# Windowed attention with a mixture of adapters on one core: pooled PSUM banks, single output groups, a written order, and the regroup copies of q and k on GpSimd

## The chip, the cores and the metric

The kernel runs on one core of a Trainium2 chip. A core has five engines that run side by side, each working through its own list in order: TensorE (PE in the profile; its weight loads, PEld, overlap its matmuls), VectorE (DVE), ScalarE (ACT), GpSimd (POOL) and SyncE (SP). In this kernel GpSimd issues every load and SyncE every store. Matrix products land in PSUM, which has 8 banks of 2 KB per partition; the other tiles lie in SBUF. The metric is the device time of one execution in microseconds, lower is better, as a median of several runs.

## The reference

Sliding-window attention over 8 batches and 8 heads, 576 positions, head size 64, and behind it a mixture of 8 adapters of rank 16 of which each row takes two:

```python
scores = scale * np.matmul(q, k.transpose(0, 1, 3, 2))
mask = np.abs(pos[:, None] - pos[None, :]) <= 32
attn = softmax(np.where(mask, scores, -1e9))
x = np.matmul(attn, v)                 # heads side by side: 4608 rows x 512
logits = x @ w_gate                    # 8 gates a row, the two largest kept, softmax over them
out = x + sum over the two kept e of w_e * (x @ A[e]) @ B[e]
```

## The kernel before, in words

The work is a list of small tasks, each with a two-letter name. A planner (`tasks`, `plan`) gives each task an engine, an assumed cost, what it depends on and a due time, schedules them on a model of the engines, and the kernel then emits them in that order. Each engine's instructions keep the order in which they are emitted, so this order is what decides who waits behind whom.

Two heads at a time are worked on: a unit `u` is one pair of heads of one batch, 32 units in all, four to a batch.

- `LD` loads a tile of 128 rows of q (`w` = 0) or k (`w` = 1), 18 tiles each, in tile `l`, cast to f16 on the way (L272). A tile that lies across two batches takes two DMAs. Six buffers each. `LV` loads half a batch of v (L279), and `SV` shifts a part of it to other partitions (L284, VectorE).
- `RG`, the regroup copy (L288): the tile holds one head of the pair behind the other; the copy, SBUF to SBUF, puts the two heads of a position side by side (tile `c`, three buffers each).
- `TR` turns `c` by eight transposes on TensorE into PSUM (L296). `EQ` copies the turned q into the ring `qR` (L305 to L309), `EK` the turned k into the ring `kR` as two copies of 64 partitions (L316, ScalarE).
- `SC` makes a tile of eight score blocks: two matmuls of 512 columns for the mask (L323) and eight score matmuls (L327). `EX` is the exponential on ScalarE (L332), into tile `PT`.
- `PV` multiplies with v and a column of ones, 13 matmuls a unit (L346); `MU` divides by the sums, a reciprocal and a product on VectorE (L355, L356), into `x`.
- Once a batch: `TX` turns `x` (L368) and `XE` copies it to `xT` (L374); `PZ` multiplies with A and the gate weights (L382); `G1`, `GA`, `G2` choose the two gates and scale (L399 to L420, on VectorE but for one exponential at L407); `TZ` and `ZE` turn the scaled result (L427, L431); `PD` multiplies with B and adds x back through the identity (L437, L440), for two groups of 128 rows at a time; `OB` copies to the output tile `ob` (L449, ScalarE) and `ST` stores it (SyncE), one store for each group of rows.

PSUM is held as three tiles `W` of two banks for scores, PV, PZ and PD, and two tiles `T` of one bank for the transposes. A batch has five groups of 128 rows, so the output of a batch goes in three steps, of two, two and one group. `ZK`, `ZV`, `ZP` write the zeros and ones that stay in `kR`, `vbd` and `PT`. The weights of the adapters are loaded by six DMAs from GpSimd behind the 16th load (L507 to L511). The constants (identity, mask) are made on GpSimd when the first transpose is emitted.

Of the kernel before, what the change touches and what calls it, by code (L numbers as in the profile page):

```python
# [49 lines left out]
class Task:  # L50
    __slots__ = ("key", "eng", "cost", "deps", "take", "give", "due", "start", "end",
                 "left", "users", "ready", "slot", "lat", "seq")

    def __init__(self, key, eng, cost, deps, take=None, give=None, lat=0.2):
        self.key, self.eng, self.cost, self.deps = key, eng, cost, deps
        self.take, self.give, self.lat = take, give, lat


OFF = {"LD": -14.73, "LV": -10.97, "RG": -16.63, "TR": -2.72, "EQ": -37.15, "EK": 25.79, "SV": 12.6,
       "SC": -0.11, "EX": 11.83, "PV": 1.3, "MU": -33.19, "TX": 3.53, "XE": -49.66, "PZ": 7.11,  # L60
       "G1": -57.49, "GA": 7.42, "G2": -66.76, "TZ": -23.09, "ZE": 10.68, "PD": 11.21, "OB": 13.67,
       "ZK": 4.21, "ZV": 30.71, "ZP": 29.46}


def tasks(off=OFF):

    ts = {}

    def add(key, u, eng, cost, deps, take=None, give=None, lat=0.2):
        t = Task(key, eng, cost, deps, take, give, lat)  # L70
        t.due = u + off[key[0]]
        t.seq = len(ts)
        ts[key] = t

# [482 lines left out]
```

## Time and profile before

| | us |
|---|---|
| median of three runs | 145.97 (145.54 to 146.17) |
| profiled execution | 147.01 |
| its span, first to last instruction | 145.0 |
| TensorE busy in the span | 119.1 |
| ScalarE busy | 111.0 |
| VectorE busy | 109.9 |
| GpSimd busy | 52.0 |

All profile lines come from one execution. "L288" is line 288 of the kernel; behind a line stand the engine, the operation, what it writes and reads, and the shapes (partitions x elements). In a group, "x36 | 14.6, 434 | 5.4 <-DMA l" is: 36 instructions, 14.6 us busy in all, 434 ns each on average, and 5.4 us for which the engine stood idle ahead of them, mostly for the load of `l`. In the timeline the first number is the start and the second how long it took. Matmuls run pipelined, so a single busy time overlaps the next one. GpSimd's DMA rows show the time to issue a load, not the transfer.

### The profile page before, as it was taken

What the parts mean: (1) busy time and instruction counts of PE and PEld (TensorE: products, weight loads), DVE (VectorE), ACT (ScalarE), POOL (GpSimd) and SP (SyncE); (2) the same over time, 40 slices, a digit from 0 to 9 for tenths busy, and PEclk for the clock granted to TensorE, in tenths of its full rate; (3) what the DMA queues carried; (4) which work ended last, traced back from release to release, by engine and by line L of the source; (5) the groups of instructions that cost most, each with busy time, mean ns of one, the idle gap of its engine ahead of it and who ended that gap; (6) DMA issues with size and microseconds to landing.
All of it is one profiled execution on the core that took longest, in us unless ns stands there. A gap on an engine that the chain in (4) does not pass through costs nothing.

```text
span 145.0 us, 4013 instructions
## 1 busy us (share of the span) xinstructions
PE 119.1 (82%) x1624; PEld 100.9 (70%) x1624; DVE 109.9 (76%) x279; ACT 111.0 (77%) x127; POOL 52.0 (36%) x80
## 2 busy tenths in 40 slices
PE   0257959796789599999999999999999999792770
PEld 0246757685677598888979788988898788582440
DVE  5769889993895989899899999989778456946000
ACT  7739877569769569999998999889979975553160
POOL 7998377589534355546256021000000000000000
PEclk9999999999999999999999999999999999999558
DMA  2999999999999999999999999924403050548035
GB/s 10 204 141 183 199 198 188 132 128 142 163 195 180 190 243 207 198 283 229 223 209 276 195 216 280 178 58 156 133 0 127 16 188 5 192 136 300 28 127 199
DMA packets 38770, 24.12 MB, mean 166 GB/s; under 512 B 24800, under 2 KB 34144, under 8 KB 38752
## 3 DMA queue, kind: packets, MB, share of 16 engines
q0 software_dynamic: 33504, 14.43, 84.1%
q1 hardware_dynamic: 5248, 9.44, 19.0%
q8 instruction: 12, 0.20, 0.5%
q14 instruction: 6, 0.05, 0.1%
HBM read 28.85 MB, written 9.44 MB: 264 GB/s over the span
## 4 chain that ended last, share of the span: by engine, by line
PE 51%; DVE 24%; issue 10%; DMA 8%; ACT 2%; POOL 1%; ACTq 0%; DVEq 0%; POOLq 0%
PE W L346 10%; DMA l<-in_q_dram 8%; PE W L323 7%; PE W L327 7%; PE T L296 6%; PE W L437 5%; PE W L382 5%; PE W L440 5%; PE T L368 4%; DVE x L356 4%; DVE c L288 4%; DVE vbd L284 3%; DVE xT L374 3%; DVE rc L355 2%; DVE zs L420 2%
## 5 line engine op out<-in xcount | busy, mean ns | idle before, releaser
L316 ACT COPY kR<-T 64x1024 f16<-64x1024 f16 x36 | 36.2, 1005 | 7.1 <-PE T L296 6.8
L332 ACT ACTIVATE PT<-W 128x1024 f16<-128x1024 f32 x36 | 35.4, 1038 | 5.5 <-PE W L327 4.6
L346 PE MATMUL W<-vbd,PT 128*128 128x130 f16 x416 | 28.6, 219 | 2.0 <-DVE vbd L284 2.0
L296 PE MATMUL T<-ident,c 128*128 128x128 f16 x288 | 22.6, 229 | 9.0 <-DVE c L288 7.7
L449 ACT COPY ob<-W 128x1024 f32<-128x1024 f32 (+1 forms) x24 | 20.9, 876 | 9.9 <-PE W L440 7.7
L356 DVE TENSOR_TENSOR x<-W,rc 128x640 f16<-128x640 f32 x32 | 26.4, 824 | 1.1
L346 PEld LDWEIGHTS <-PT 128*128 128x128 f16 x416 | 25.0, 97 | 2.3 <-DVE vbd L284 2.3
L327 PEld LDWEIGHTS <-kR 128*128 128x128 f16 x288 | 19.5, 99 | 8.9 <-issue 0.7
L296 PEld LDWEIGHTS <-c 128*128 128x128 f16 x288 | 18.7, 103 | 9.7 <-DVE c L288 9.6
L323 PE MATMUL W<-identQ,mask 128*128 128x512 f16 x72 | 22.0, 387 | 2.7 <-DVE x L356 2.7
L327 PE MATMUL W<-qR,kR 128*128 128x128 f16 x288 | 22.4, 222 | 0.0
L272 POOL DMA_DIRECT2D l<-in_k_dram x24 | 15.9, 665 | 10.5 <-DMA l<-in_k_dram 3.1
L279 POOL DMA_DIRECT2D vbd<-in_v_dram x16 | 13.3, 835 | 16.0 <-PE T L427 7.4
L272 POOL DMA_DIRECT2D l<-in_q_dram x24 | 16.4, 683 | 7.0 <-DMA l<-in_k_dram 1.9
L288 DVE COPY c<-l 128x1024 f16<-128x1024 f16 x36 | 14.6, 434 | 5.4 <-DMA l<-in_k_dram 4.5
L440 PEld LDWEIGHTS <-xT 128*128 128x128 f16 x160 | 13.3, 104 | 7.1 <-issue 2.8
L437 PE MATMUL W<-B_sb,zT 128*128 128x512 f16 x40 | 16.4, 410 | 1.8 <-ACT zT L431 0.8
L374 DVE COPY xT<-T 128x1024 f16<-128x1024 f16 (+1 forms) x24 | 13.4, 598 | 4.6 <-PE T L368 3.8
L440 PE MATMUL W<-ident,xT 128*128 128x128 f16 x160 | 16.7, 231 | 0.0
L368 PE MATMUL T<-ident,x 128*128 128x128 f16 x160 | 11.8, 219 | 3.0 <-DVE xT L374 1.5
L284 DVE COPY vbd<-vbd 32x2304 f16<-32x2304 f16 x16 | 12.7, 794 | 0.7 <-DMA vbd<-in_v_dram 0.3
L368 PEld LDWEIGHTS <-x 128*128 128x128 f16 x160 | 9.8, 98 | 3.6 <-DVE x L356 1.7
(49 smaller groups left out, 115.5 us busy)
## 6 DMA issues: line engine op xcount, KB each, us to landing
out_dram<-ob SPq DMA_DIRECT2D x24, 256.0 KB, 2.9
vbd<-in_v_dram POOLq DMA_DIRECT2D x16, 288.0 KB, 9.4
l<-in_q_dram POOLq DMA_DIRECT2D x12, 256.0 KB, 9.6
l<-in_k_dram POOLq DMA_DIRECT2D x12, 256.0 KB, 9.9
out_dram<-ob SPq DMA_DIRECT2D x16, 192.0 KB, 2.9
l<-in_q_dram POOLq DMA_DIRECT2D x4, 192.0 KB, 7.6
l<-in_k_dram POOLq DMA_DIRECT2D x4, 192.0 KB, 7.3
l<-in_q_dram POOLq DMA_DIRECT2D x4, 128.0 KB, 9.1
```

The lines of the kernel that those rows point to most:

```text
L272: keep(nc.gpsimd.dma_start(out=raw[w][t % NRAW][f - FT * t:f - FT * t + n], in_=src[f - NF * b:f - NF * b + n]))
L296: keep(nc.tensor.matmul(out=tp[:, FT * slot:FT * slot + FT], lhsT=src[:, j, :], rhs=ident, is_transpose=True, start=True, stop=True))
L316: keep(nc.scalar.copy(out=dst.rearrange("p a (r f j) -> p a r f j", r=2, j=4), in_=kt[64 * o:64 * o + 64]))
L323: keep(nc.tensor.matmul(out=p[:, i:i + 4], lhsT=maskT, rhs=bcast(identQ, 1, 4), start=True, stop=False))
L327: keep(nc.tensor.matmul(out=p[:, i], lhsT=kR[:, a, :], rhs=qR[:, :, 8 * a:8 * a + 16], start=False, stop=(i % 4 == 3)))
L332: keep(nc.scalar.activation(out=PTs[T % NPT][:, :, 64:192].rearrange("p i (f j) -> p i f j", j=J), in_=ps("SC", T).rearrange("p (i j f) -> ...
L346: keep(nc.tensor.matmul(out=po[:, GS * g:GS * g + 2 * VD], lhsT=PTs[T % NPT][:, sl, off:off + 128], rhs=rhs[:, :, V0 - 1:V0 + D], start=(i ...
L356: keep(nc.vector.tensor_tensor(out=xs[b % NX].rearrange("p g (h n d) -> p g h n d", h=2, n=NP)[:, :, :, n], in0=pog[:, :, :, 1:VD], in1=bc ...
L368: keep(nc.tensor.matmul(out=tp[:, c0:c0 + 128], lhsT=xs[b % NX][:, g, 128 * c:128 * c + 128], rhs=ident, is_transpose=True, start=True, st ...
L437: keep(nc.tensor.matmul(out=pd[:, i], lhsT=zTs[b % 2][:, g], rhs=B_sb, start=True, stop=False))
L440: keep(nc.tensor.matmul(out=pd[:, i, 128 * c:128 * c + 128], lhsT=xTs[b % NXT][:, g, c], rhs=ident, start=False, stop=(c == 3)))
L449: keep(nc.scalar.copy(out=dst, in_=src))
```

## The change

- **Order.** The planner goes. A fixed text `ORDER` names the tasks in the order of emission. Behind a colon stands the PSUM bank (0 to 7) that a TensorE task writes, or the engine (A for ScalarE, D for VectorE) of a copy.
- **PSUM.** Four tiles of two banks serve everything; each task takes the bank or the pair of banks that `ORDER` names.
- **Regroup copies.** `RG` of tiles 0 and 1 stays on VectorE; the other 32 run on GpSimd, in the queue that also issues the loads.
- **Buffers.** Load tiles 4 in place of 6 for each of q and k, `xT` 3 in place of 2, and the output 7 tiles of one group in place of 3 of two.
- **Engines.** `EQ` is 14 times on VectorE and 4 times on ScalarE (9 and 9 before); of the 36 copies of `EK` 4 are on VectorE, and the two halves are separate tasks; `XE` is 16 times on VectorE and 10 on ScalarE (24 and 0); `ZE` in halves both ways; `ZV` 3 and 3.
- **Output.** `PD`, `OB` and `ST` go by single groups: 29 output copies on ScalarE and 11 on VectorE.
- **Last batch.** `MU` of the last unit, `PZ`, the scaling, `TZ` and `ZE` come in two parts (groups 0 to 2, then 3 and 4); `TX` and `XE` by single groups; and the residual matmuls (`PX`) come ahead of the product with B (`PB`).
- **Start.** The identity is made ahead of the first load; the other constants and the weights' loads have places of their own in the order. One gate step (`is2`, L414 before) moves from G2 to G1.

```diff
-NV, NPT, NRAW, NCAST, NX, NXT, NOB = 3, 4, 6, 3, 2, 2, 3
-NW, NTP = 3, 2
+NV, NPT, NRAW, NCAST, NX, NXT, NOB = 3, 4, 4, 3, 2, 3, 7
+NW = 4
+LB = B - 1
...
+ORDER = """
+CI ZK.1 LD.0.0 LD.0.1 ZP.0 LD.1.0 ZP.3 ZV.1.0:A LV.0.0 ZP.2 ZP.1 LD.1.1 Z1.1 Z1.2 CQ ZK.3 CM
+ZV.0.0:A RG.0.0 WB ZK.0 TR.0.0:0 LD.2.0 ZV.1.1:D EQ.0:A RG.1.0 LD.2.1 ZV.2.0:A RG.0.1 TR.1.0:0
+ZK.4 LV.0.1 TR.0.1:1 Z1.0 RG.1.1 WA EQ.1:D EK.0.0:A TR.1.1:2 ZV.0.1:D EK.0.1:A SV.0.0 EK.1.1:A
+SC.0:0 ZK.2 EK.1.0:A RG.2.0 SC.1:4 ZV.2.1:D EX.0 SC.2:2 RG.2.1 SV.0.1 EX.1 TR.2.0:6 LD.3.0
+TR.2.1:7 EQ.2:D LD.3.1 EX.2 PV.0:4 EK.2.1:D LD.4.0 SC.3:0 EK.2.0:A MU.0 PV.1:2 LV.1.0 EX.3
+SC.4:6 LV.1.1 MU.1 PV.2:0 RG.3.0 EX.4 MU.2 RG.3.1 TR.3.0:6 PV.3:2 EQ.3:D RG.4.0 TR.3.1:0 MU.3
+SC.5:6 EK.3.1:A LD.4.1 SV.1.0 TX.0.1:1 EX.5 TX.0.2:2 LD.5.0 TX.0.0:3 XE.0.2:D TR.4.0:4 XE.0.1:A
+LD.5.1 XE.0.0:D LV.2.0 EQ.4:D EK.3.0:A PZ.0:2 LD.6.0 SV.1.1 SC.7:0 G1.0 RG.4.1 PV.4:4 EX.7
+RG.5.0 TR.4.1:6 MU.4 GA.0 SC.6:0 EK.4.0:A RG.5.1 G2.0 TR.5.0:7 EX.6 LD.6.1 TR.5.1:4 EK.4.1:A
+PV.6:0 EQ.5:D LV.2.1 PV.5:2 EK.5.0:A MU.6 RG.6.0 SC.8:6 EK.5.1:A SV.2.0 LD.7.0 TZ.0:5 SC.9:0
+MU.5 ZE.0:A LD.7.1 TR.6.0:4 EX.8 RG.6.1 PD.0.1:5 EQ.6:D SC.10:2 EX.9 LD.8.0 SV.2.1 TR.6.1:4
+LD.8.1 EX.10 PV.7:6 EK.6.1:D LV.3.0 SC.11:0 OB.0.1:A RG.7.0 EK.6.0:A MU.7 ST.0.1.1 PV.8:2 RG.7.1
+EX.11 TR.7.0:5 MU.8 TX.1.2:4 TX.1.1:6 RG.8.0 EQ.7:A TX.1.0:7 XE.1.1:D TR.7.1:2 RG.8.1 XE.1.0:A
+XE.1.2:D SC.12:0 PV.9:4 LD.9.0 EX.12 PZ.1:6 LD.9.1 MU.9 EK.7.1:A LD.10.0 PV.10:0 G1.1 LD.10.1
+EK.7.0:A PD.0.2:3 LV.3.1 SC.13:4 OB.0.2:A MU.10 LV.4.0 GA.1 TR.8.1:2 ST.0.2.2 EX.13 G2.1
+TR.8.0:3 RG.9.0 SC.14:0 EK.8.1:A RG.9.1 PV.11:4 EQ.8:D EX.14 TZ.1:6 RG.10.0 MU.11 PD.0.3:7
+ZE.1:A PD.0.0:3 PD.0.4:0 RG.10.1 SV.3.0 OB.0.0:A TX.2.0:1 OB.0.4:A TX.2.1:6 ST.0.0.0 XE.2.0:D
+LV.5.0 EK.8.0:A TX.2.2:3 ST.0.4.4 SC.15:4 XE.2.2:D LV.5.1 XE.2.1:D OB.0.3:A TR.9.0:3 EX.15
+LV.4.1 SV.3.1 TR.9.1:2 ST.0.3.3 SC.16:6 EQ.9:D LD.11.0 EK.9.1:A PV.13:4 SV.4.0 EX.16 LD.11.1
+PV.12:0 MU.13 TR.10.1:3 EK.9.0:A PZ.2:6 LD.12.0 MU.12 EK.10.0:A LD.12.1 SC.17:4 LD.13.0 G1.2
+EK.10.1:A PD.1.2:2 TR.10.0:0 LD.13.1 OB.1.2:D GA.2 PD.1.1:1 EX.17 G2.2 PD.1.4:3 ST.1.2.7
+PD.1.0:2 LD.14.0 OB.1.4:A PV.15:4 RG.11.0 OB.1.0:A ST.1.4.9 PD.1.3:3 OB.1.1:A EQ.10:D ST.1.0.5
+TZ.2:2 RG.11.1 OB.1.3:A SC.18:6 ST.1.1.6 SV.4.1 ZE.2:A ST.1.3.8 PV.14:0 RG.12.0 MU.15 EX.18
+TR.11.1:2 TR.11.0:3 RG.12.1 MU.14 EK.11.1:A SC.19:6 EQ.11:D RG.13.0 TX.3.0:0 EX.19 SV.5.1
+TX.3.2:1 TX.3.1:3 LD.14.1 SC.20:4 XE.3.2:D XE.3.1:A RG.13.1 XE.3.0:D PV.16:6 EX.20 SV.5.0
+RG.14.0 SC.21:0 MU.16 PV.17:4 EX.21 LV.6.0 EK.11.0:D TR.12.1:3 RG.14.1 PZ.3:6 EK.12.1:A MU.17
+LD.15.0 PV.18:0 EK.12.0:A G1.3 PD.2.1:2 LD.15.1 TR.12.0:4 OB.2.1:A PD.2.0:5 MU.18 GA.3 SC.22:2
+ST.2.1.11 EQ.12:A LD.16.0 G2.3 TR.13.0:0 LD.16.1 OB.2.0:A PD.2.2:1 EX.22 LD.17.0 ST.2.0.10
+SC.23:4 RG.15.0 EQ.13:D TZ.3:6 EX.23 PV.19:2 OB.2.2:D RG.15.1 TR.13.1:7 ZE.3:D ST.2.2.12 PV.20:4
+MU.19 EK.13.1:A LV.7.1 SC.24:0 RG.16.0 MU.20 TX.4.0:6 EX.24 TX.4.2:2 RG.16.1 SV.6.0 TX.4.1:3
+PD.2.3:4 XE.4.0:A XE.4.1:D TR.14.0:5 LV.7.0 PD.2.4:0 XE.4.2:D OB.2.3:A TR.14.1:6 EQ.14:D RG.17.0
+OB.2.4:A PV.21:2 ST.2.3.13 EK.14.1:A EK.13.0:D ST.2.4.14 LD.17.1 SC.25:4 LV.6.1 EK.14.0:A PZ.4:0
+MU.21 EX.25 SV.7.1 SC.27:6 G1.4 PV.22:4 EX.27 RG.17.1 SC.26:2 MU.22 GA.4 SC.28:6 EX.26 G2.4
+TR.15.0:4 EX.28 TR.16.0:5 PD.3.2:2 EQ.16:D TR.15.1:3 EQ.15:A TZ.4:6 OB.3.2:D PD.3.4:7 PD.3.1:5
+EK.15.0:A ZE.4:D ST.3.2.17 PV.23:0 OB.3.4:D EK.15.1:A PD.3.3:2 SV.6.1 ST.3.4.19 SC.29:6 OB.3.3:A
+MU.23 PD.3.0:4 EX.29 ST.3.3.18 PV.24:2 OB.3.1:D TX.5.0:0 OB.3.0:A MU.24 ST.3.1.16 TX.5.2:1
+TX.5.1:5 ST.3.0.15 XE.5.2:A PV.25:6 XE.5.0:D XE.5.1:A TR.16.1:1 MU.25 SC.30:2 EK.16.0:A SV.7.0
+PZ.5:4 EX.30 PD.4.0:0 EK.16.1:A G1.5 PV.26:2 OB.4.0:A SC.31:6 MU.26 GA.5 ST.4.0.20 PD.4.2:0
+EX.31 G2.5 TR.17.1:1 PD.4.4:2 OB.4.2:A PD.4.3:3 OB.4.4:A PV.27:6 ST.4.2.22 OB.4.3:A ST.4.4.24
+TZ.5:0 MU.27 EK.17.1:A SC.32:4 ST.4.3.23 TR.17.0:3 EX.32 TX.6.2:2 EQ.17:D TX.6.1:6 TX.6.0:7
+XE.6.1:A XE.6.2:D SC.33:4 XE.6.0:D EK.17.0:A PV.28:2 PZ.6:6 EX.33 MU.28 ZE.5:A PD.4.1:1 G1.6
+PV.29:2 OB.4.1:A SC.34:4 ST.4.1.21 MU.29 GA.6 SC.35:0 EX.34 G2.6 PD.5.0:2 EX.35 PV.30:4 PD.5.2:3
+OB.5.0:A MU.30 TZ.6:0 OB.5.2:A PV.31:6 ST.5.0.25 ZE.6:D ST.5.2.27 PD.5.1:4 MA.31 PD.5.4:5
+OB.5.1:A PD.6.0:0 MB.31 OB.5.4:A TX.7.0:1 ST.5.1.26 OB.6.0:D TX.7.1:4 TX.7.2:6 ST.5.4.29
+XE.7.1:A TX.7.4:7 XE.7.0:D TX.7.3:5 ST.6.0.30 PD.5.3:0 XE.7.2:D XE.7.3:A PD.6.1:1 OB.5.3:D
+XE.7.4:A PZa.7:2 OB.6.1:A ST.5.3.28 PZb.7 ST.6.1.31 PD.6.2:1 G1.7 PD.6.4:0 OB.6.2:A PX.7.0:6
+OB.6.4:D ST.6.2.32 PX.7.1:4 GA.7 G2a.7 PD.6.3:1 ST.6.4.34 G2b.7 TZa.7:0 ZEa.7:D TZb.7:2 OB.6.3:D
+ZEb.7:A PB.7.0 PB.7.1 OB.7.0:A OB.7.1:D ST.6.3.33 PX.7.2:0 PB.7.2 OB.7.3:A OB.7.2:D ST.7.0.99
+ST.7.1.99 ST.7.3.99 OB.7.4:A ST.7.2.99 ST.7.4.99
+"""
...
-    obs = many(NOB, [128, 2, DD], F32, "ob")
+    obs = many(NOB, [128, DD], F32, "ob")
...
+    def ps(*key):
+        return Ws[int(where[key]) // 2]
+    def bank(*key):
+        i = int(where[key])
+        return Ws[i // 2][:, 512 * (i % 2):512 * (i % 2) + 512]
+    def bank16(*key):
+        return bank(*key).bitcast(F16)
+    def copy_on(*key):
+        return nc.scalar.copy if where[key] == "A" else nc.vector.tensor_copy
...
     def RG(t, w):
-        keep(nc.vector.tensor_copy(out=cst[w][t % NCAST],
-                                   in_=raw[w][t % NRAW].rearrange("p o (j d) -> p j o d", j=J)))
+        copy = nc.vector.tensor_copy if t < 2 else nc.gpsimd.tensor_copy
+        keep(copy(out=cst[w][t % NCAST],
+                  in_=raw[w][t % NRAW].rearrange("p o (j d) -> p j o d", j=J)))
...
+    def MA(u):
+        recip(u)
+        mult(u, 0, 3)
+    def MB(u):
+        mult(u, 3, NG)
+    def gs(b, h):
+        return range(h, h + 1) if b == LB else range(2 * h, min(NG, 2 * h + 2))
...
+    def delta(b, g, pd, **kw):
+        keep(nc.tensor.matmul(out=pd, lhsT=zTs[b % 2][:, g], rhs=B_sb, **kw))
+    def resid(b, g, pd, first):
+        for c in range(4):
+            keep(nc.tensor.matmul(out=pd[:, 128 * c:128 * c + 128], lhsT=xTs[b % NXT][:, g, c],
+                                  rhs=ident, start=(first and c == 0),
+                                  stop=(not first and c == 3)))
+    def PD(b, g):
+        delta(b, g, bank("PD", b, g), start=True, stop=False)
+        resid(b, g, bank("PD", b, g), False)
+    def PX(b, h):
+        for g in range(2 * h, min(NG, 2 * h + 2)):
+            resid(b, g, half(b, g), True)
+    def PB(b, h):
+        for g in range(2 * h, min(NG, 2 * h + 2)):
+            delta(b, g, half(b, g), start=False, stop=True)
+    def OB(b, g):
+        src = half(b, g) if b == LB else bank("PD", b, g)
+        keep(copy_on("OB", b, g)(out=obs[(NG * b + g) % NOB], in_=src))
...
-    loads = 0
-    for t in order:
-        if t.key[0] == "TR" and t.key[1:] == (0, 0):
-            constants()
-        do[t.key[0]](*t.key[1:])
...
+    pieces = locals()
+    for name, *nums in order:
+        pieces[name](*nums)
```

More of the change, by code (lines that the diff above doesn't have):

```diff
@@ new lines, in pz, with proj, PZa, PZb @@
+    def pz(b):
+        return ps(*(("PZa", b) if b == LB else ("PZ", b)))
+    def proj(b, g0, g1):
+        for g in range(g0, g1):
+            for c in range(4):
+                keep(nc.tensor.matmul(out=pz(b)[:, GS * g:GS * g + ER + E],
+                                      lhsT=xTs[b % NXT][:, g, c, :], rhs=WA_sb[:, c, :],
+                                      start=(c == 0), stop=(c == 3)))
+    def PZ(b):
+        proj(b, 0, NG)
+    def PZa(b):
+        proj(b, 0, 3)
+    def PZb(b):
+        proj(b, 3, NG)
```

347 lines of the change are left out of this document (96 added, 251 removed).

## The prediction

> **What bounds the kernel now.** I read the page's busy shares first, then busy time by stage, then the chain of waits. The page:
>
> ```profile
> span 145.0 us, 4013 instructions
> PE 119.1 (82%) x1624; PEld 100.9 (70%) x1624; DVE 109.9 (76%) x279; ACT 111.0 (77%) x127; POOL 52.0 (36%) x80
> ```
>
> Three engines stand near 110 us, so no average names the bound. Busy time by stage does (columns: window, length, then busy us of PE, weight loads, DVE, ACT, POOL; clock; DMA share; GB/s):
>
> ```profile
> 0.00:49.40 49.40, 33.46 (x433) 28.00 (x434) 39.24 (x93) 37.80 (x38) 34.30 (x56) 1.00 1.45 160
> 49.40:120.00 70.60, 70.14 (x1025) 61.15 (x1023) 60.91 (x156) 62.83 (x75) 17.72 (x25) 1.00 0.97 179
> 120.00:145.00 25.00, 15.54 (x174) 11.77 (x171) 9.76 (x32) 10.36 (x14) 0.00 (x0) 0.85 0.42 143
> ```
>
> From 49.4 to 120 us TensorE never rests. It loses time ahead of that, while q and k arrive, and behind it, in the last batch. The chain of waits inside the full stage gives what each piece of TensorE work costs there (start, us, what):
>
> ```profile
> 97.15 0.45 PE W L327 x8
> 97.59 0.45 PE T L296 x8
> 98.04 0.22 PE W L437
> 98.26 0.22 PE W L440 x4
> 99.37 0.75 PE W L346 x13
> 100.11 0.43 PE W L323 x2
> 100.99 0.28 PE T L427 x5
> 102.79 0.89 PE T L368 x16
> 106.73 1.18 PE W L382 x20
> ```
>
> All of it: 36 transposes (TR) of 0.45, 36 score tiles (SC) of 0.43 + 0.45, 32 PV of 0.75, 8 TX of 1.11 (0.89 for 16 matmuls, so for 20), 8 PZ of 1.18, 8 TZ of 0.28, 40 output groups (PD) of 0.44: 110.0 us, the same before and after. So the span is 110.0 plus what TensorE loses, 35.0. When PV.8 starts at 49.4, the written order has put 28.8 us of work behind it (15 TR, 13 SC, 8 PV, 2 TX, PZ, TZ, two PD groups): 20.6 lost by then, 14.4 after.
>
> **The copies on GpSimd, the term that decides.** Of 36 regroup copies 32 leave VectorE and join the queue that issues every load. GpSimd's own rows:
>
> ```profile
> L272 POOL DMA_DIRECT2D l<-in_q_dram x24 | 16.4, 683 | 7.0 <-DMA l<-in_k_dram 1.9 <-DMA l<-in_q_dram 1.5 <-DVE gate L418 1.1
> L279 POOL DMA_DIRECT2D vbd<-in_v_dram x16 | 13.3, 835 | 16.0 <-PE T L427 7.4 <-PE W L346 3.5 <-DMA vbd<-in_v_dram 3.4
> L507 POOL DMA_DIRECT2D WA_sb<-in_moe_A_dram x4 | 3.5, 899 | 0.0
> L472 POOL COPY identQ<-ident 128x128 f16<-128x128 f16 x1 | 0.4, 403 | 0.1
> L475 POOL TENSOR_SCALAR_AFFINE_SELECT mask<-mask 128x128 f16<-128x128 f16 x1 | 0.3, 317 | 0.1
> masks.py:199 POOL TENSOR_SCALAR_AFFINE_SELECT ident<-ident 128x128 f16<-128x128 f16 x1 | 0.3, 287 | 0.1
> masks.py:197 POOL MEMSET ident<- 128x128 f16 x1 | 0.2, 231 | 0.0
> L541 POOL MEMSET const-float32-0.0<- 128x1 f32 x1 | 0.1, 98 | 0.2 <-issue 0.2
> ```
>
> No row shows a copy of 128x1024, so its price c is bounded. One element costs 98 ns, 128 elements add 133 (memset), 189 to 219 (select) or 305 (the copy, which reads with a stride); times 8, plus 98: 1.16, 1.61 to 1.85 (middle 1.73), or 2.54 us. Nothing excludes two f16 a step, half the memset's slope: 0.63. The regroup copy reads runs of 64 and computes nothing, so it lies below select and nearest to memset: I take 1.25 and keep 0.63 and 2.54. The Trainium skill (GPSIMD Engine Reference, § 3.1 and § 4.1) says one-input work runs near line rate, 1.03 cycles an element for light bodies: by that an estimate of c = 0.98. The Trainium skill's same page, § 7, has 1.9 cycles against 2.9 once a read steps over 8 bytes; the strided copy's 305 ns fit the 2.9, and 1.9 would be an estimate of c = 1.72. By the sum below the two give 136 and 149 us.
>
> Now GpSimd's queue as the new order has it, up to the copy RG.7.0. The start and the split loads:
>
> ```profile
> 1.25 0.84 POOL L272 DMA_DIRECT2D l<-in_q_dram  x1 [0.80 <-POOLq L541]
> 6.16 1.17 POOL L272 DMA_DIRECT2D l<-in_q_dram  x2
> DMA to landing us min/median/max: 3.7/9.2/13.1
> l<-in_k_dram POOLq DMA_DIRECT2D x2, 256.0 KB, 5.0
> ```
>
> Start 1.25; constants 1.9, now partly ahead of the first load; 12 whole loads of 0.70, 6 split ones of 1.2, 7 v loads of 0.83, the weights 3.5 and 1.4 (two more issues): 29.4 us, plus 11c. A copy also waits here for its load, with the next loads queued behind it and the transposes waiting for it. The shortest distances, LD.3.0 to RG.3.0 and LD.4.1 to RG.4.1, hold 4.2 and 4.6 us of issues against 3.7 to 5.0 to landing: 1.0 us for both. TR.7.0 can start at 30.5 + 11c = 44.3. TensorE has 26.6 us ahead of it (14 TR, 12 SC, 9 PV, TX, PZ, TZ, one PD): 17.7 lost, against 20.6 now.
>
> From RG.7.0 to RG.11.1 the queue holds 13.9 us of issues (4 whole and 4 split q and k loads more or less: 2.8 + 2.4 + 1.4 + 2.4 + 0.7, and 5 v loads of 0.83) and 9c: 25.1. TensorE has 24.1 us from TR.7.0 to TR.11.1 (8 TR, 2 TX, 7 SC, 7 PV, 2 PZ, 2 TZ, 9 PD). It waits 1.0 there. Beyond, the copies run ahead: to RG.13.1 another 0.7 + 4c against 13.5 us of work. The later waits for v buffers hold only copies that are early. LD.17.1 stands 1.5 us ahead of its copy and makes it late, by about 3 us; 12.8 us of other work lies between that transpose and the last PV. Four load buffers in place of six cost nothing: LD.t waits for RG.t-4, which stands ahead of it in the same queue.
>
> **VectorE, ScalarE and the banks.** Rows by shape:
>
> ```profile
> L288 DVE COPY c<-l 128x1024 f16<-128x1024 f16 x36 | 14.6, 434 | 5.4 <-DMA l<-in_k_dram 4.5 <-DMA l<-in_q_dram 0.7
> L316 ACT COPY kR<-T 64x1024 f16<-64x1024 f16 x36 | 36.2, 1005 | 7.1 <-PE T L296 6.8
> L374 DVE COPY xT<-T 128x1024 f16<-128x1024 f16 x16 | 10.5, 688 | 4.1 <-PE T L368 3.4 <-ACT ob L449 0.5
> L449 ACT COPY ob<-W 128x512 f32<-128x512 f32 x8 | 4.8, 596 | 1.4 <-PE W L440 1.3
> L493 ACT COPY vbd<-zero 64x2376 f16<-64x2376 f16 x2 | 4.3, 2175 | 0.0
> L284 DVE COPY vbd<-vbd 32x2304 f16<-32x2304 f16 x16 | 12.7, 794 | 0.7 <-DMA vbd<-in_v_dram 0.3
> ```
>
> VectorE sheds 32 x 0.434 = 13.9 and 8 large xT copies, 5.5. It takes 11 single output groups at 0.69 (the time of as many bytes in the xT row; no row has the form, ends 0.5 and 0.8), 4 kR copies at 0.69 to 1.0, 5 qR and 3 zT copies: about 16. ScalarE's output goes from 20.9 us to 29 x 0.596 = 17.3; it loses 4 kR, 5 qR and half of the zT copies, about 12, and gains 10 xT copies, 8.5, and a zeroing copy, 2.2. Both end some 4 us lower, off the path while TensorE is full: nothing. If that cover went, they would be worth their 4 us. Pooling eight banks and seven single output tiles removes waits that the full stage doesn't show: nothing. SP issues the same 40 stores. The gate step that goes from G2 to G1, the parts of the constants and the reordered zeroing are the same instructions at other places: nothing.
>
> One cost speaks against the move. VectorE still has instructions with both ends in SBUF, 16 v shifts and five gate steps a batch with two SBUF inputs, about 41 of them while copies run. If each met a running copy and waited for half of it: copies fill 40 of some 85 us, 41 x 0.47 x 0.63 = 12 us of waiting on VectorE, at most 41 x 1.25 = 51. VectorE has 70.6 - 60.9 = 9.7 us free in the full stage. I take 1.0 on the path; ends 0 and 12. The Trainium skill (SBUF — State Buffer, § Who interferes with whom) states such a lock: GpSimd's port is VectorE's second, and whoever comes second is blocked for the whole instruction. No row here shows it, since GpSimd ran no long copy.
>
> **The last batch.** Rows of the timeline:
>
> ```profile
> 124.19 0.91 PE L346 MATMUL W<-vbd,PT 128*128 128x130 f16 x13
> 126.11 0.82 DVE L356 TENSOR_TENSOR x<-W,rc 128x640 f16<-128x640 f32 x1
> 126.99 1.01 PE L368 MATMUL T<-ident,x 128*128 128x128 f16 x15 [0.48 <-DVE x L356]
> 129.82 1.35 PE L382 MATMUL W<-WA_sb,xT 128*128 128x136 f16 x20
> 133.54 0.82 DVE L420 TENSOR_TENSOR zs<-W,gate 128x640 f16<-128x640 f32 x1
> 135.18 0.69 ACT L431 COPY zT<-T 128x640 f16<-128x640 f16 x1 [2.64 <-PE T L427]
> 135.92 0.61 PE L437 MATMUL W<-B_sb,zT 128*128 128x512 f16 x1 [0.78 <-ACT zT L431]
> 139.60 1.50 ACT L449 COPY ob<-W 128x1024 f32<-128x1024 f32 x2 [0.69 <-PE W L440]
> ```
>
> Last PV end to first TX is 1.9 us, as the product waits behind batch 6's gates; after them, with three of five groups, some 1.0: saves 0.9. TX to the end of PZ is 4.2; copies on two engines make it 3.2: saves 1.0. Product zs, TZ and zT in two parts save 0.5. From the end of zT to the last output copy 5.2 us pass (135.9 to 141.1); the residual half is now done ahead, and five single copies on two engines leave 0.8 + 3 x 0.6: saves 2.7. Sum 5.1. Eight PD groups stand behind the last PV instead of five; they fill waits.
>
> **The sum.** 110.0 + 17.7 + 1.0 + (14.4 - 5.1) + 1.0 = 139.0 us of span against 145.0. The profiled execution took 147.0 with 2.0 outside the span; the median of the runs shown is 145.97, 0.97 above the span. So 140.0. In c: 125.2 + 11c + 9c - 10.2, the last two terms only where positive.
>
> **The rivals.** *The copy is dear and GpSimd becomes the bound* (slower): place, the queue ahead of TR.7 and TR.11; from c = 1.55 the sum passes 145.97; 149.6 at the select's 1.73, 166 at the strided copy's 2.54. For it speaks that the only copy row is the dearest; against it, its stride. Chance 0.18. *VectorE waits for GpSimd* (the lock): 4 to 12 instead of 1.0, 143 to 151; from 7.0 it decides. For it, 41 instructions; against, 9.7 us free. Chance 0.20. *The head gains nothing*, because ScalarE, with three zeroing copies ahead of the first kR copies, sets the start: only the last batch, 145.97 - 5.1 + 1 = 142. Against it, 11.6 us idle of 49.4 on ScalarE now. Chance 0.10. *The copy is cheap*, c from 0.63 to 1.1: 132 to 137. Chance 0.12. The forecast itself, c from 1.1 to 1.45: 137 to 144. Chance 0.40.
>
> **How the numbers follow.** Half a per cent, 0.7 us, is about what a measurement can tell. Faster: 0.40 + 0.12 + 0.10 + 0.12 of the lock = 0.74; within 0.5%: 0.03 of the lock, 0.02 of the dear copy, 0.05; slower: 0.21. The range 133.5 to 151 leaves out the cheapest copies (0.05) and copies above 1.8 us (0.09). For the likeliest alone it is 137 to 144.
>
> **What would show it.** A GpSimd copy row between 1.1 and 1.45 us; TR.7.0 near 44 us; TensorE full from there but for a gap of a microsecond at TR.11; VectorE's v shifts still near 0.79 us; 11 us from the last PV to the last output copy's end instead of 16. It is wrong if the copy row is above 1.55, if v shifts and gate steps take twice as long, or if TensorE has gaps between 50 and 115 us.

## The result, and the profile after

| | us |
|---|---|
| kernel before, median of 4 runs beside the change | 145.75 (145.33 to 146.17) |
| changed kernel, median of 4 runs | 159.38 (157.22 to 159.93) |
| ratio | 1.084, 95% interval 1.073 to 1.096 |
| profiled execution of the changed kernel, its span | 159.85, 158.1 |

The change makes the kernel 8.4% slower; 140.0 was predicted, at most 151. Ratios, and the times in the sections below, leave out runs more than 1.5% above the fastest of their kernel (of the changed kernel 157.22 and 158.90 stay, median 158.06), while the ranges show every run, and a ratio compares runs taken side by side, so that it need not be the quotient of two medians. The page of the changed kernel, with the same columns as before:

```profile
span 158.1 us, 4022 instructions
...
PE 121.8 (77%) x1624; PEld 101.1 (64%) x1624; DVE 114.2 (72%) x265; ACT 106.6 (67%) x130; POOL 86.4 (55%) x112
```

GpSimd took on 34 us of work, and yet no engine is busier than 77%. Busy time by stage shows where TensorE loses:

```profile
0.00:49.40 49.40, 34.04 (x412) 27.88 (x413) 37.93 (x81) 34.63 (x34) 41.22 (x59) 1.00 1.31 135
49.40:120.00 70.60, 59.11 (x836) 50.11 (x833) 52.91 (x118) 49.95 (x63) 45.14 (x54) 1.00 1.09 177
120.00:158.00 38.00, 28.65 (x383) 23.11 (x380) 23.37 (x67) 21.98 (x34) 0.00 (x0) 0.96 0.38 130
```

The stage that was full, 70.14 of 70.60 us, is full no more: 11.5 us of it are gaps, and VectorE and ScalarE have both become *less* busy there (60.9 to 52.9, 62.8 to 50.0). All three wait, for each other and for loads. The groups of the new copy and of two VectorE steps (a v shift was 794 ns, this gate step 167 ns):

```profile
L182 POOL COPY c<-l 128x1024 f16<-128x1024 f16 x32 | 34.0, 1070 | 20.3 <-DMA l<-in_k_dram 6.6 <-DMA l<-in_q_dram 6.2 <-PE W L190 4.8
...
L177 DVE COPY vbd<-vbd 32x2304 f16<-32x2304 f16 x16 | 15.6, 978 | 4.8 <-DMA vbd<-in_v_dram 4.4
...
L326 DVE TENSOR_TENSOR dm<-m,m 128x5 f32<-128x5 f32 x8 | 2.1, 262 | 0.3
```

The copy is cheap, 1.07 us on average. And the table of waits (who, for whom, us in total, times, longest) has rows between pairs that the kernel before has no row for; L190 is TR, L199 and L203 EQ, L209 EK, L285 XE, L389 PD, L415 OB:

```profile
ACT kR L209 <- DVE qR L199: 2.8, 1, 2.8
...
PE W L389 <- ACT kR L209: 2.1, 4, 0.8
...
ACT ob L415 <- DVE xT L285: 1.7, 1, 1.7
```

A k eviction waits for a q eviction, an output product for a k eviction, an output copy for an xT copy. No data goes from the one to the other. What they share is a two-bank tile of PSUM, of which each uses a bank of its own. Set beside the banks that `ORDER` names, nine of TensorE's fifteen waits in this stage, 5.6 of its 11.5 us of gaps, end with an engine that read the *other* bank of the same tile. Four more, 4.4 us, end with one that read the bank itself, and two, 1.3 us, with a late v shift and a late copy.

To set it against the prediction: the copy RG.7.0 starts at 47.57 and TR.7.0 at 48.66; the last PV ends at 139.82 and the last output copy at 152.89 (rows of the timeline):

```profile
47.57 1.04 POOL L182 COPY c<-l 128x1024 f16<-128x1024 f16 x1 [0.98 <-DMA l<-in_q_dram]
...
48.66 0.62 PE L190 MATMUL W<-ident,c 128*128 128x128 f16 x8 [0.80 <-POOL c L182]
...
138.91 0.91 PE L239 MATMUL W<-vbd,PT 128*128 128x130 f16 x13
...
151.60 1.29 DVE L415 COPY ob<-W 128x512 f32<-128x512 f32 x2 [0.72 <-ACT ob L415]
```

With the prediction's 110.0 us of TensorE work, and 6.1 us of it (8 PD, TX, PZ, TZ) behind the last PV, the span falls apart like this:

| TensorE's loss | predicted | measured | |
|---|---|---|---|
| up to TR.7.0 | 17.7 | 22.1 | 48.66 less 26.6 of work |
| from there to the last PV | 1.0 + 1.0 | 13.8 | the rest |
| behind the last PV | 9.3 | 12.2 | 158.1 - 139.82 - 6.1 |
| span | 139.0 | 158.1 | |

Of 19.1 us of error 11.8 lie in the middle.

### The profile page after: what moved, and what is told of

Same layout as the page of the kernel before. It is cut to its first block, busy times and chain, and to the rows that moved or that the text cites. A ratio compares the mean times of both kernels' runs of the same rounds, so it can differ in the third digit from the quotient of the medians.

```text
span 158.1 us, 4022 instructions
## 1 busy us (share of the span) xinstructions
PE 121.8 (77%) x1624; PEld 101.1 (64%) x1624; DVE 114.2 (72%) x265; ACT 106.6 (67%) x130; POOL 86.4 (55%) x112
## 4 chain that ended last, share of the span: by engine, by line
PE 28%; DMA 27%; ACT 15%; DVE 11%; POOL 9%; issue 5%; DVEq 1%; POOLq 0%; ACTq 0%
DMA l<-in_k_dram 16%; DMA vbd<-in_v_dram 11%; ACT kR L209 8%; POOL l L165 5%; PE W L239 4%; PE W L190 4%; PE W L216 4%; PE W L389 4%; PE W L220 4%; POOL c L182 3%; PE W L279 3%; DVE vbd L177 3%; PE W L393 3%; ACT ob L415 3%; ACT PT L225 3%
## 5 line engine op out<-in xcount | busy, mean ns | idle before, releaser
L182 POOL COPY c<-l 128x1024 f16<-128x1024 f16 x32 | 34.0, 1070 | 20.3 <-DMA l<-in_k_dram 6.6
L209 ACT COPY kR<-W 64x1024 f16<-64x1024 f16 x32 | 32.0, 1006 | 14.1 <-PE W L190 4.6
L190 PE MATMUL W<-ident,c 128*128 128x128 f16 x288 | 22.7, 230 | 15.3 <-DVE c L182 10.6
L190 PEld LDWEIGHTS <-c 128*128 128x128 f16 x288 | 19.0, 104 | 17.0 <-DVE c L182 11.1
L256 DVE TENSOR_TENSOR x<-W,rc 128x640 f16<-128x640 f32 (+2 forms) x33 | 26.4, 804 | 1.1
L415 ACT COPY ob<-W 128x512 f32<-128x512 f32 x29 | 16.2, 589 | 11.4 <-PE W L393 6.6
L177 DVE COPY vbd<-vbd 32x2304 f16<-32x2304 f16 x16 | 15.6, 978 | 4.8 <-DMA vbd<-in_v_dram 4.4
L389 PE MATMUL W<-B_sb,zT 128*128 128x512 f16 x40 | 14.6, 378 | 4.7 <-ACT kR L209 2.1
L165 POOL DMA_DIRECT2D l<-in_k_dram x24 | 16.4, 687 | 1.6 <-DMA vbd<-in_v_dram 1.3
L172 POOL DMA_DIRECT2D vbd<-in_v_dram x16 | 13.8, 868 | 2.4 <-DMA vbd<-in_v_dram 2.0
L393 PE MATMUL W<-ident,xT 128*128 128x128 f16 x160 | 14.8, 219 | 0.0
L199 DVE COPY qR<-W 128x1024 f16<-128x1024 f16 x14 | 9.6, 687 | 6.1 <-PE W L190 2.8
L279 PE MATMUL W<-ident,x 128*128 128x128 f16 x160 | 10.9, 219 | 3.9 <-DVE x L256 1.7
```

Of the source, the lines that this page charges most:

```text
L165: keep(nc.gpsimd.dma_start(out=raw[w][t % NRAW][f - FT * t:f - FT * t + n], in_=src[f - NF * b:f - NF * b + n]))
L182: keep(copy(out=cst[w][t % NCAST], in_=raw[w][t % NRAW].rearrange("p o (j d) -> p j o d", j=J)))
L190: keep(nc.tensor.matmul(out=tp[:, FT * slot:FT * slot + FT], lhsT=src[:, j, :], rhs=ident, is_transpose=True, start=True, stop=True))
L209: keep(copy_on("EK", t, o)(out=dst.rearrange("p a (r f j) -> p a r f j", r=2, j=4), in_=kt[64 * o:64 * o + 64]))
L256: keep(nc.vector.tensor_tensor(out=xg[:, g0:g1, :, n], in0=pog[:, :, :, 1:VD], in1=bcast(rcs[u][:, g0:g1], 3, D), op=ALU.mult))
L279: keep(nc.tensor.matmul(out=tp[:, c0:c0 + 128], lhsT=xs[b % NX][:, g, 128 * c:128 * c + 128], rhs=ident, is_transpose=True, start=True, st ...
```

## The experiments

Theory 1: the copies stand in the queue of the loads and wait for landings there. Theory 2: GpSimd is simply full. Theory 3: not the copies but the rest of the change costs the time. Theory 4, made after the first four runs: the pooled tiles do, since the waits that the program sets go by tile and not by bank, and so tie the two banks of a tile together.

**The copies back on VectorE, in the changed kernel.**

```diff
-        copy = nc.vector.tensor_copy if t < 2 else nc.gpsimd.tensor_copy
+        copy = nc.vector.tensor_copy
```

> The changed kernel with one part undone: all 36 regroup copies on VectorE, everything else as changed. Theory 1 (the copies sit in the queue that issues the loads and wait there for a load to land, so the next loads go out late; the last copy ends at 113 us where it ended at 96 before): loads go out as soon as a buffer is free, VectorE takes 32 x 0.43 = 14 us more, and the time falls from 159 to 144 to 149 us. Theory 2 (GpSimd is simply full: 86 us of issues and copies): the same fall, so this run doesn't tell 1 from 2. Theory 3 (the copies are harmless; the written order, four load buffers in place of six or the pooled banks cost the time): 155 us or more.

156.06 us (155.44 to 156.3), 1.070 of before (1.062 to 1.077). Only 2.0 us come back; 10 are due to the rest of the change. Theory 3.

**The loads three tiles ahead, in the changed kernel.** Each `LD.t` from the third tile on stands behind `RG.t-3`, the weights behind `RG.3.1`.

```diff
-    for word in ORDER.split():
+    words = ORDER.split()
...
+        behind = f"RG.{int(t) - 3}.{x}"
...
+    for word in words:
```

> The changed kernel, copies on GpSimd as changed, but each load of tile t is put right behind the copy of tile t-3 in the order (as early as four buffers allow), and the weights' loads go behind the third tile's copies. No work is added or taken away. Theory 1: a copy finds its load landed, the 12.8 us for which GpSimd's copies wait for loads shrink below 5, and the time falls to 144 to 150 us. Theory 2: GpSimd's work is the same 86 us, so the time stays at 155 us or more. Theory 3: stays at 155 or more unless it is the place of the loads in the order.

156.9 us in the profiled run, 162.72 to 164.35 in the other three; one run is too few for a ratio. It is 0.3 us below the fastest run of the changed kernel and far from theory 1's 144 to 150, although no copy on GpSimd waits for a load any more (12.8 us before this edit). GpSimd's share of the chain of waits goes from 9 to 32%: what is issued earlier in its queue stands ahead of copies and v loads.

**Loads left out, in the changed kernel.**

```diff
     for name, *nums in order:
+        if name == "LD" and nums[0] >= 4 or name == "LV" and nums[0] >= NV:
+            continue
         pieces[name](*nums)
```

> The changed kernel without the loads of q and k from tile 4 on and of v from batch 3 on: the copies read what already lies in the buffers, so most of the attention is computed from the wrong rows. It shows what all the rest of the change takes when nothing waits for a transfer. Theory 1 and theory 2: 136 to 142 us, the time that the prediction gave for copies that are never late (their row says 1.04 us, which by its sum is 137). Theory 3: 150 us or more.

156.0 us in one run. With hardly a load left to wait for (DMA share 0.19 in the stage from 49.4 to 120 us), TensorE still has 8.3 us of gaps there:

```profile
49.40:120.00 70.60, 62.29 (x886) 53.14 (x883) 56.81 (x127) 52.97 (x66) 16.64 (x16) 1.00 0.19 65
```

Of these gaps 5.5 us end with an engine that read the other bank of the same tile. With the ties in place, theories 1 and 2 explain some 2 us of the changed kernel's time.

**The copies on GpSimd, in the kernel before.**

```diff
-        keep(nc.vector.tensor_copy(out=cst[w][t % NCAST],
+        copy = nc.vector.tensor_copy if t < 2 else nc.gpsimd.tensor_copy
+        keep(copy(out=cst[w][t % NCAST],
```

> The kernel before with one part of the change alone: the regroup copies from tile 2 on on GpSimd, in the order of the planner. Theory 1: the copies block later loads in the queue here too, though six buffers and another order put the loads further ahead: 150 to 158 us. Theory 2: 52 + 34 = 86 us of GpSimd work inside 96 us of loading: 148 us or more. Theory 3: within 1 us of 145.8, or faster, since VectorE loses 14 us of work.

160.48 us (159.56 to 166.11), 1.099 of before (1.086 to 1.113). So the copies alone cost the kernel before 14.5 us, and the rest alone 10, while both together cost 12.3: two limits, of which each covers a part of the other.

**One tile for the two transposes, in the kernel before.** The clean test of theory 4: the same instructions in the same order, two banks as before, declared as halves of one tile.

```diff
-    Ts = [psum.tile([128, 1024], F16, name=f"T{i}") for i in range(NTP)]
+    TT = psum.tile([128, 2048], F16, name="T")
+    Ts = [TT[:, 1024 * i:1024 * i + 1024] for i in range(NTP)]
```

> The kernel before, with the same instructions in the same order and in the same banks; only the two one-bank tiles of the transposes are declared as the halves of one two-bank tile, as the single-bank pieces lie in the changed kernel. Theory 4 (a two-bank tile ties its two banks together: whoever writes or reads one bank waits for whoever reads or writes the other): every frame tile then has its k transposes behind the q eviction and its halves one behind another, 16 frame tiles at 0.5 us or more: 152 us or above. Theory 3 as the order written out (the changed order loses the time, the banks do not): 146, as before.

164.35 us (163.37 to 165.05), 1.128 of before (1.120 to 1.135): a declaration costs 18 us. Its waits (L306 EQ, L317 EK, L369 TX, L428 TZ):

```profile
DVE qR L306 <- ACT kR L317: 4.0, 4, 1.4
...
PE T L297 <- ACT qR L306: 3.1, 1, 3.1
...
PE T L428 <- ACT kR L317: 2.2, 2, 1.4
...
PE T L369 <- ACT zT L432: 1.6, 2, 0.9
```

And one place of its timeline, where the q eviction stands until the k eviction of the other bank ends:

```profile
61.08 2.01 ACT L317 COPY kR<-T 64x1024 f16<-64x1024 f16 x2
...
63.12 0.69 DVE L306 COPY qR<-T 128x1024 f16<-128x1024 f16 x1 [0.68 <-ACT kR L317]
...
63.87 0.44 PE L428 MATMUL T<-ident,zs 128*128 128x128 f16 x5 [0.33 <-DVE qR L306]
```

In the kernel before the same two run side by side:

```profile
64.10 2.02 ACT L316 COPY kR<-T 64x1024 f16<-64x1024 f16 x2
64.49 0.69 DVE L305 COPY qR<-T 128x1024 f16<-128x1024 f16 x1
```

Set beside the banks that the planner gave, 16.9 us of TensorE's idle time in this run end with an engine that read the other of the two banks; in the kernel before none does. Theory 4 holds, and the price is larger than its lower bound of 6. The Trainium skill (PSUM — Partial Sum Buffer, § PSUM bank collisions raise a hardware error) has engines in different banks run clean side by side. By that nothing in the chip asks for these waits; they are the program's own.

**Untied banks in the changed kernel.** Every engine's order stays; the banks are given out anew, by going through the order's list with three two-bank tiles and two one-bank tiles, so that a tile holds one task at a time (45 of 106 single-bank tasks take a two-bank tile alone).

```diff
-NW = 4
+NW, NTP = 3, 2
...
+    Ts = [psum.tile([128, 512], F32, name=f"T{i}") for i in range(NTP)]
...
+        if i >= 2 * NW:
+            return Ts[i - 2 * NW][:, 0:512]
```

> The changed kernel with every engine's order as it is, and only the banks given out anew: three two-bank tiles and two one-bank tiles, as in the kernel before, and where a single-bank piece stands in a two-bank tile it has it alone. Theory 4: the time that the ties cost comes back, some 8 of the 10 us that the changed kernel loses without its copies' cost: 148 to 153. Theory 3 as the order: no gain, 157 to 162, or worse since two banks fewer are free at a time.

156.56 us (155.88 to 159.31), 1.075 of before (1.066 to 1.084): 1.5 us of gain, a miss. With the copies on VectorE as well:

> The same as the last, with the regroup copies on VectorE. Theory 4: 144 to 149, near the kernel before. Theory 3 as the order: 154 to 158, as the changed kernel had with its copies on VectorE (156.06).

150.42 us (149.14 to 150.98), 1.031 of before (1.024 to 1.038): between the two forecasts, so both missed. The four kernels in one table:

| us | copies on VectorE | copies on GpSimd | difference |
|---|---|---|---|
| tied banks | 156.06 | 158.06 | 2.0 |
| untied banks | 150.42 | 156.56 | 6.1 |
| difference | 5.6 | 1.5 | |

The ties cost 5.6 us and the copies 6.1; beside the other each shows only a part. The 5.6 are what is left of the gain after 45 tasks take two banks each in place of one. 4.6 us to the kernel before remain (4.4 by the medians of all runs, which the forecasts below use). In this run TensorE's gaps in the stage from 49.4 to 120 us are 5.9 us, against 0.5 in the kernel before:

```profile
49.40:120.00 70.60, 64.75 (x917) 55.14 (x915) 62.82 (x154) 55.80 (x72) 18.99 (x27) 1.00 0.91 165
```

Eleven waits make up 5.4 of them, and each is for a bank that another engine still reads; a tie is no longer among them.

**What remains: the loads, the buffers, the engines?** Three runs on the untied kernel with the copies on VectorE. First six load buffers, with the loads issued three to five tiles ahead:

```diff
-NV, NPT, NRAW, NCAST, NX, NXT, NOB = 3, 4, 4, 3, 2, 3, 7
+NV, NPT, NRAW, NCAST, NX, NXT, NOB = 3, 4, 6, 3, 2, 3, 7
...
+        behind = f"RG.{int(t) - min(5, max(3, int(t) // 2))}.{x}"
```

> The changed kernel with three two-bank and two one-bank tiles and the copies on VectorE (150.42), and with six load buffers in place of four, each load issued three to five frame tiles ahead. If the 4.4 us that this still lacks to the kernel before come from the loads (VectorE and GpSimd wait for them, and the chain gives 28 per cent to transfers): 145 to 148. If they come from the order written out: 150 to 152.

153.92 us (153.79 to 156.6), 1.058 of before (1.048 to 1.068): worse than both forecasts, and not a test of the buffers alone, since loads that wait for a free buffer now hold the v loads up. So the buffers alone, with nothing moved:

```diff
-NV, NPT, NRAW, NCAST, NX, NXT, NOB = 3, 4, 4, 3, 2, 3, 7
+NV, NPT, NRAW, NCAST, NX, NXT, NOB = 3, 4, 6, 3, 2, 3, 7
```

> The changed kernel with untied banks and the copies on VectorE (150.42), with six load buffers in place of four and nothing moved. If four buffers hold the loads up (GpSimd's load issues waited some 9 us for buffers there): 147 to 149. If the order written out sets it: 149.5 to 151.

150.03 us (149.6 to 151.29), 1.030 of before (1.025 to 1.036): no difference to 150.42. Then q, k, xT, zT and output evictions on the engines of the kernel before (`EQ` by turns, `EK` and `OB` on ScalarE, `XE` on VectorE):

```diff
-EQ.3:D EK.2.1:D XE.1.0:A ZE.3:D OB.2.2:D
...
+EQ.3:A EK.2.1:A XE.1.0:D ZE.3:A OB.2.2:A
...
```

> The changed kernel with untied banks and the copies on VectorE (150.42), and with the evictions of q, k, xT, zT and the output of the first seven batches on the engines that the kernel before uses; VectorE falls by some 12 us to 110. If VectorE's load is what the 4.4 us are: 146 to 148. If it is the order in which TensorE's pieces stand: 149.5 to 153.

151.37 us (151.21 to 151.51), 1.038 of before (1.032 to 1.045), with VectorE down from 122.0 to 111.2 us. Not the engines either. By elimination the 4.6 us lie in the order in which the pieces stand, in the output by single groups, which all these runs keep, and in how often a bank is waited for under this assignment. The eleven waits above speak for the banks in the middle of the kernel; the three were not separated by a run.

**Where GpSimd's copies cost.** Three runs on the kernel before. With the later loads left out (q and k behind the first six pairs, v behind three batches):

```diff
+        if t.key[0] == "LD" and t.key[1] >= NRAW or t.key[0] == "LV" and t.key[1] >= NV:
+            continue
         do[t.key[0]](*t.key[1:])
```

> The kernel before with the regroup copies on GpSimd (162.14), and with the loads of q and k behind the first six pairs and of v behind the first three batches left out (so it computes from old data); the copies stay. Theory 1 (the copies stand in the queue of the loads, and each waits for landings): the whole loss goes, 143 to 149. Theory 2 (GpSimd's own time, and the slower shifts beside it): 84.8 us of GpSimd work falls to some 53, and a part of the loss stays: 150 to 156. Theory 4 says nothing of this run.

156.24 us in one run: some 4 of the 14.5 us go, 10 stay. Theory 1 is not the whole of it. VectorE's steps beside the copies stay long in this run: the gate step of 167 ns takes 633 on average, a v shift 878 in place of 794. With only the frame tiles 8 to 17 on GpSimd:

```diff
+        copy = nc.vector.tensor_copy if t < 8 else nc.gpsimd.tensor_copy
```

> The kernel before with the regroup copies of the frame tiles 8 to 17 alone on GpSimd, 20 of the 32 that cost it 16 us. If the cost lies in the head, where the copies stand between the load issues of GpSimd's queue and TensorE is starved by what comes late (theories 1 and 2 alike, before 50 us): 145 to 148. If every copy costs, by its 1.07 us and the slower shifts and gate steps beside it: 20 of 32 parts of 16, 153 to 158.

152.92 us (152.57 to 155.02), 1.056 of before (1.045 to 1.066). 20 of 32 copies, none of them before 43 us, cost 6.5 to 8 us. The chain of waits names one piece above all, a v load that was issued at 85.75 us, where the same load left at 76.14 in the kernel before, and landed 10.5 us later. Ahead of it in the queue stand copies, of which some waited for loads of their own (the second fence is from the table of waits):

```profile
85.75 10.52 DMA vbd<-in_v_dram
```

```profile
POOL c L289 <- DMA l<-in_q_dram: 13.8, 4, 7.0
```

Then copies that stand before nothing and that nobody waits for, 20 of the same form behind the last load:

```diff
+            if loads == 2 * NTT + 2 * B:
+                for s in spare:
+                    keep(nc.gpsimd.memset(s, 0.0))
+                for _ in range(20):
+                    keep(nc.gpsimd.tensor_copy(out=spare[1],
+                                               in_=spare[0].rearrange("p o (j d) -> p j o d", j=J)))
```

> The kernel before with 20 copies of the regroup's form on GpSimd behind its last load, of data that nobody reads, so that they stand before nothing and nobody waits for them: some 21 us of GpSimd work between about 82 and 104 us, where TensorE is full. If the running beside VectorE costs by itself (small gate steps of 0.17 us took 0.39 to 0.63 in the mean beside such copies): 148.5 or more. If only the queue costs, in which the copies wait for loads and later loads wait behind them: 145.5 to 147.

154.63 us (153.95 to 154.83), 1.058 of before (1.055 to 1.062). The idle work, 23.1 us of copies and 1.9 us of two memsets that zero their tiles first, costs 8.6 us by running alone. The groups between 85 and 105 us, first of the kernel before, then of this one:

```profile
L284 DVE COPY vbd<-vbd 32x2304 f16<-32x2304 f16 x5 | 4.0, 802 | 0.1
...
L374 DVE COPY xT<-T 128x1024 f16<-128x1024 f16 x4 | 2.6, 687 | 0.9 <-PE T L368 0.9
...
L288 DVE COPY c<-l 128x1024 f16<-128x1024 f16 x5 | 2.0, 418 | 0.0
...
L419 DVE TENSOR_TENSOR gate<-gate,s 128x40 f32<-128x40 f32 x1 | 0.2, 202 | 0.0
```

```profile
L290 DVE COPY c<-l 128x1024 f16<-128x1024 f16 x3 | 4.2, 1408 | 0.0
L286 DVE COPY vbd<-vbd 32x2304 f16<-32x2304 f16 x3 | 3.9, 1297 | 0.1
...
L376 DVE COPY xT<-T 128x1024 f16<-128x1024 f16 x2 | 1.3, 686 | 0.0
...
L421 DVE TENSOR_TENSOR gate<-gate,s 128x40 f32<-128x40 f32 x1 | 1.1, 1067 | 0.0
```

VectorE's steps from SBUF to SBUF take longer, those that read PSUM don't. Five steps of the gate chain took 0.92 to 1.07 us each, where they take 0.16 to 0.20 in the kernel before; the difference is nearly a whole GpSimd copy of 1.04. The mean of the regroup copies (L290) hides three different ones: beside the idle copies two took 0.83 and 0.41 us, and the third took 2.98, beside two load issues and the two memsets:

```profile
85.14 2.98 DVE L290 COPY c<-l 128x1024 f16<-128x1024 f16 x1
85.97 1.86 POOL L526 MEMSET spare<- 128x1024 f16 x2
88.14 2.99 DVE L286 COPY vbd<-vbd 32x2304 f16<-32x2304 f16 x2
91.91 0.38 PE L370 MATMUL T<-ident,x 128*128 128x128 f16 x4 [3.62 <-DVE xT L376]
```

This copy and the two shifts behind it hold up the copy xT for which TensorE stands 3.62 us. So the memsets have a part in the 8.6 us; how large, no run separates.

**The last batch alone, in the kernel before.** The planner's order is kept up to the last store but one of batch 5, and a list written out does the rest, in the manner of the changed kernel; every piece has a tile to itself.

```diff
+TAIL = """
+MA.31 MB.31 TZ.6 OB.5.2 ZE.6 ST.5.2 TX.7.0:T0 PD.6.0 TX.7.1:T1 XE.7.0:D XE.7.1:A TX.7.2:T0 OB.6.0
+XE.7.2:D TX.7.3:T1 XE.7.3:A TX.7.4:T0 XE.7.4:D ST.6.0 PZa.7:W1 PD.6.1 PZb.7 G1.7 OB.6.1 PD.6.2
...
+"""
```

> The kernel before with the changed kernel's last batch alone (single groups, residual ahead of the gates, five copies by two engines), each piece in a tile that no other piece holds at that time. From the last score-times-v product's end to the span's end the kernel before takes 19.9 us, the changed kernel 18.3, and the changed kernel with banks that are not tied 16.4. If the finer last batch is worth what the banks did not take from it, 3.5 us: 142.5, between 140.5 and 144.5. If it is worth nothing by itself: 146.

144.77 us (143.94 to 145.72), 0.991 of before (0.987 to 0.996): a part of it, and just above the range expected. Here the gate chain starts only at 132.69. In another order, five transposes first and the gates' product ahead of two of batch 6's output products:

```diff
-MA.31 MB.31 TZ.6 OB.5.2 ZE.6 ST.5.2 TX.7.0:T0 PD.6.0 TX.7.1:T1 XE.7.0:D XE.7.1:A TX.7.2:T0 OB.6.0
-XE.7.2:D TX.7.3:T1 XE.7.3:A TX.7.4:T0 XE.7.4:D ST.6.0 PZa.7:W1 PD.6.1 PZb.7 G1.7 OB.6.1 PD.6.2
+MA.31 MB.31 TZ.6 TX.7.0:T0 OB.5.2 ZE.6 ST.5.2 XE.7.0:D TX.7.1:W2 XE.7.1:A TX.7.2:T1 XE.7.2:D
+TX.7.3:W0 XE.7.3:A TX.7.4:T0 XE.7.4:D PD.6.0 OB.6.0 ST.6.0 PZa.7:W1 PZb.7 G1.7 PD.6.1 PD.6.2 GA.7
...
```

> The kernel before with the finer last batch (144.77), its pieces in another order: the five groups are transposed one behind another ahead of the output products of batch 6, and the gates' products ahead of two of these, so that the gate chain starts when its own inputs are there (in the last run it started 1.6 us after VectorE had become idle). If that chain sets the end: 1.5 to 2 us less, 142.5 to 143.5. If the stores at the end set it: 144 to 145, no change.

142.94 us (142.18 to 144.98), 0.980 of before (0.974 to 0.985), the fastest version on record, about 2% below the kernel before. Three rows of its timeline, the first TX, the gate chain's first step and the last output copies:

```profile
126.88 0.22 PE L508 MATMUL T<-ident,x 128*128 128x128 f16 x1
...
130.91 0.20 DVE L416 TENSOR_REDUCE m<-W 128x5 f32<-128x40 f32 x1 [1.64 <-PE W L519]
...
135.90 1.29 DVE L580 COPY last<-W 128x512 f32<-128x512 f32 x2 [1.29 <-PE W L576]
```

## Why the prediction was wrong, step by step

- **"Pooling eight banks and seven single output tiles removes waits that the full stage doesn't show: nothing."** This step failed. The pooling also *adds* waits, between pieces that only share a tile, and they were not looked for. In the full stage 5.6 us of TensorE's gaps are such waits. With the copies on VectorE, untying gives back 5.6 us, with the copies on GpSimd 1.5; the same kind of tie put into the kernel before costs 18. No rival named it.
- **VectorE and ScalarE "off the path while TensorE is full: nothing".** The condition is stated and the cover goes, but their price was put at their busy time, 4 us. What counted was who waits for whom: they got less busy and the time longer.
- **The order.** It was costed only by GpSimd's queue and by work counts. 4.6 us of loss stay with it and with the single output groups when ties, copies, buffers and evictions are taken out. Load buffers "cost nothing": right, 150.03 against 150.42.
- **The copy's price**, 1.25, ends 0.63 and 2.54: measured 1.07, 1.04 in the median. On the cheap side; the rival of a dear copy falls, and the prediction's own formula would have given 136 to 137 us with it. The Trainium skill's estimate in the prediction (GPSIMD Engine Reference, § 3.1 and § 4.1), 0.98, was the nearest; the trace agrees with that rule, and not with the dearer one of § 7, 1.72.
- **The queue up to RG.7.0.** Busy time right: without the 1.25 us of the start, which are idle, 28.2 + 11 x 1.04 = 39.6 were predicted with the copy's measured price, and 40.7 were measured up to the end of RG.7.0 at 48.61. Its waits were put at 1.0 us beside the 1.25, and 7.9 us of that stretch are idle. The landings were taken at 3.7 to 5.0 us. 3.7 was the shortest of q and k in the kernel before, whose median stood beside it, 9.2; in the changed kernel the whole loads took 6.2 (q), 6.3 (k) and 7.5 (v) in the median. TR.7.0 stood at 48.66, not at 44.3. "Beyond, the copies run ahead" failed as well: copies still wait for landings at 96 and 103 us.
- **The lock**, 1.0 on the path, ends 0 and 12. In the changed kernel VectorE pays some 4 us (16 shifts 0.18 longer, and the gate steps); what of it is on the path was not measured there. As a rival it was right in kind, and its 4 to 12 fit what 25 us of idle GpSimd work cost in the full stage of the kernel before, 8.6. The Trainium skill's rule (SBUF — State Buffer, § Who interferes with whom) agrees with the rows, down to the steps that read PSUM and are spared.
- **The last batch**, 5.1: from the last PV to the span's end 19.9 us became 18.3, so 1.6. Untied it is 3.5 (16.4), and in the kernel before, in the second order, 3.4 (125.7 to 142.2). The mechanism was right. Two terms were off: from the first TX to the end of PZ it took 4.0 us in that run and not 3.2, and from the last output copy to the span's end 5.0 us pass where 3.9 passed before, with five stores for the batch in both, which was not counted. The output term was right: 2.6 us from the end of zT's first part to the last copy against 2.5.

Of the signs of being wrong that the prediction named, the one that came true is "if TensorE has gaps between 50 and 115 us".

## What to carry to other kernels

Where storage is pooled, list for each tile who writes and who reads which part of it: if waits go by tile, two pieces that share nothing else will wait for each other, so a piece that is evicted by itself wants a tile by itself. Work put on GpSimd is paid for twice beyond its own time, by what stands behind it in its queue (here every load) and by VectorE's steps from SBUF to SBUF beside it; it belongs beside VectorE work that reads PSUM. And "hidden while the bound engine is full" is a statement on the kernel before: ask of every part of the change whether it keeps that engine full.

## What the runs showed of the hardware that was not expected

One gap of TensorE cost more than the gap itself. In the run with idle copies it stood for 3.6 us ahead of 91.9, and the clock granted to it was half for three of the microseconds that followed, with 12 matmuls in each where 21 ran once it was whole again (windows of 1 us):

```profile
93.00:94.00 1.00, 1.00 (x12) 1.00 (x11) 0.96 (x2) 0.00 (x0) 0.94 (x2) 0.50 0.42 42
...
95.00:96.00 1.00, 1.00 (x12) 1.00 (x11) 0.53 (x2) 0.99 (x2) 0.94 (x2) 0.50 0.00 0
...
97.00:98.00 1.00, 1.00 (x21) 1.00 (x18) 1.00 (x2) 0.73 (x1) 0.95 (x1) 1.00 0.00 0
```

So a part of that run's 8.6 us, some 1.7 us at this place (the clock stands at 0.50 from 93 to 96 and little under 1 on both sides), is the clock's. The Trainium skill (TensorE: Matmul & The Clock Gate, § What's actually happening) describes it: half rate after an idle window of about 3.4 us, and as long to come back; the trace agrees. The changed kernel ran its stage from 49.4 to 120 us at a clock of 1.00 in spite of 11.5 us of gaps; the longest of TensorE's waits there is 1.7 us.
